# A fused attention and feed-forward kernel: attention output laid over spent columns of the normed x, longer rings, and a new order of the work

## The chip, the cores and the metric

The kernel runs on one core of a Trainium2 chip. The core has several engines that run side by side, each with an instruction stream of its own: TensorE (PE in the profile: matrix multiplications, with weight loads as PEld), VectorE (DVE), ScalarE (ACT), GpSimd (POOL) and SyncE (SP, which here only starts transfers). Sixteen DMA engines move data between the chip's memory (HBM) and the two memories on the core: SBUF, where operands lie, and PSUM, where matmuls leave their sums, in eight banks. Engines wait for one another through semaphores.

The metric is the device time of one execution in microseconds (us), from first to last instruction with what lies around it; smaller is better.

## The reference

From x [1, 2048, 448] in bf16 two branches are computed, from the same normed x, and joined:

```python
xn = layernorm(x)                                   # over the 448 columns
# A: 16 heads of 28, each query sees 8 keys, at distances 0, 2, 4, ... 14 back
q, k, v = split(xn @ wqkv)                          # wqkv [448, 1344]
logits = einsum("bhsd,bhswd->bhsw", q, k[idx]) * 28 ** -0.5   # idx = pos - 2 * arange(8)
o = einsum("bhsw,bhswd->bhsd", softmax(where(idx >= 0, logits, -1e9)), v[idx])
s = o @ wo                                          # wo [448, 448]
# B: feed-forward
h = gelu(xn @ w1 + b1)                              # w1 [448, 1792]
g = silu(h @ w2 + b2)                               # w2 [1792, 448]
out = x + s * g
```

## The kernel before

**Tiling.** Since attention reaches back in steps of 2, even and odd tokens never meet. The kernel sorts them: the first 1024 positions are the even tokens, the second 1024 the odd ones, and within each half the eight keys are neighbours. Positions are cut in 16 tiles of 128 (NT), and 4 chunks of 512 (CH); chunks 0 and 1 are the even half. Attention goes through the positions in 9 visits of 4 x 57 queries.

**Stages.** Each tile of x is loaded, its statistics are taken (`stats`, lines 446 and 451; `rstds`, lines 459 to 469: for the later tiles POOL computes the root and the reciprocal, lines 468 and 469), it is normed (line 481) and transposed into `xnT` (columns by tokens; by TensorE at the start, later by a transposing DMA, line 400). Of it `qk_rows` and `vproj` make queries, keys and values (matmuls of lines 582 and 605), which are cast out of PSUM by ACT (line 334) or by VectorE (line 336). Queries and keys are turned into `qkT` by a transposing DMA (line 400); values go to HBM and back in another layout (line 392). For a visit, `spread` copies keys into `kd` (line 642 on ACT, 644 on VectorE), `scores_of` multiplies (line 757), `weights_of` takes the exponential into a buffer `E` (line 766, ACT) and masks it (line 772, VectorE), and `values_of` multiplies with the values (line 786). `output_of` divides by the sum: transpose (line 795), reciprocal (799), transpose (804), multiply (809), all on VectorE; the multiply writes attention output into `oT` and frees the PSUM bank. The feed-forward runs chunk by chunk: `ff1` (matmul in line 658, gelu on ACT in line 662), then `ff2` (line 690), `gate` (lines 724 to 740) and `final`/`gated` (matmul with wo in line 870, line 897).

**Pairs of half arrays.** The 448 rows that a matmul sums over are 3.5 times 128. `pair` (line 521) therefore runs two jobs beside each other on the upper and the lower 64 rows of the array: a first half of the work for both (four steps of two matmuls), then a second half (three steps of two), in which the two jobs have changed places. Between the two halves TensorE's results of the first must be complete. This is told by a no-op on another engine: it waits for the last matmul of the first half, and the first matmul of the second half waits for it. That engine is POOL:

```python
        def f2(k):
            held["told"] = (nc.gpsimd if k.on == "POOL" else nc.sync).nop()
            for i in held["last"]:
                behind(held["told"], i)
        told = plan.add(HOPS[0] if early else HOPS[1], 0.06, f2, [u], 300)
```

To fill the time between, the halves of neighbouring pairs are interleaved. POOL has other work in the same stream: masks and constants at the start, the roots of lines 468 and 469, some moves of values, and the loads of wo (nine transfers, and two copies within SBUF, issued in line 377 through `dma`).

**What sets the order.** All instructions are first entered as tasks in a plan (`_Plan`). A task has an engine (or a choice of engines, as the casts have, and the moves of values between SP and POOL), a cost, the tasks it depends on, buffers that it takes and gives back, and a priority: a base from `PRIO` by kind and number, plus an entry of `LATER` for the kind of step, plus an entry of `NUDGE` for single tasks by number. The planner plays the tasks through with its costs: among those that can start at about the same time on an engine it takes the one of the highest priority. Buffers are rings (`ring`): `E` has 8, `kd` 2. The instructions are then emitted in the planned order, and each engine runs its own in that order. A changed priority or ring thus moves instructions on all engines, and changes which engine gets a cast, though the code of each step stays.

SP's transfers share eight semaphores in turn, so that each waits for the one eight places ahead of it.

Of the kernel before, what the change touches and what calls it, by code (L numbers as in the profile page):

```python
# [17 lines left out]
TILED = 30  # L18
BURST = 3.5
NUDGE = {  # L20
    140: -82, 155: -215, 164: -68, 167: -111, 224: 188, 279: -38, 288: 225, 645: -245, 658: -217,
    783: -170,
}
LAST = 352
SAME = 20
# [154 lines left out]
def kernel(  # L180
# [13 lines left out]
    P = 128  # L194
    S, D, H, DH, F = A_x.shape[1], 448, 16, 28, 1792
# [4 lines left out]
    KT = 4  # L200
# [5 lines left out]
    G = 4  # L206
    HALF = S // 2


    NW, NK, BACK, PAD = 57, 64, 7, 16  # L210
# [22 lines left out]
    def sb(name, shape, dt=BF16):  # L233
        return const.tile(shape, dt, name=name)
# [10 lines left out]
    b1r = sb("b1r", [P, P])  # L245
    b1 = sb("b1", [P, NMT], F32)
    b2 = sb("b2", [P, D])
    xnT = sb("xnT", [P, KT, S])
    qkT = sb("qkT", [P, 2, G, PAD + S])
    v_tok = [sb(f"v_tok{t}", [P, 2, H // 2, 32]) for t in range(4)]  # L250
    v_hbm = dram.tile([BACK + S, H * 32], BF16, name="v_hbm")
    oT = sb("oT", [P, KT, S])
    o_hbm = dram.tile([NCH, 60, CH], BF16, name="o_hbm")
    ident = sb("ident", [P, P])
    eps_t = sb("eps_t", [P, 1], F32)
# [10 lines left out]
    def ring(name, n, shape, dt=BF16, fifo=False):  # L266
        return _Pool([sb(f"{name}{i}", shape, dt) for i in range(n)], fifo)

    p_xn = ring("xn", 4, [P, 512])
    p_st = ring("st", 4, [P, 6], F32)  # L270
    p_E = ring("E", 8, [P, 8 * NW], fifo=True)
    p_dt = ring("dt", 2, [P, 480], F32)
    p_rd = ring("rd", 2, [P, H], F32)
    p_y = ring("y", 2, [P, D], F32)
# [6 lines left out]
    p_g.bufs = p_g.bufs + late_g  # L281
    p_h = ring("h", 28, [P, CH], fifo=True)
    p_v = ring("v", 3, [P, 4, H // 2, 32], fifo=True)
    p_k = ring("kd", 2, [P, G, 4, 2 * NK], fifo=True)
    qk_tok = [sb(f"qk_tok{i}", [P, 2, H, 32]) for i in range(4)]
    p_f = _Pool([None])
    p_q = _Pool([None] * QUEUE)
# [1 line left out]


    PRIO = {
        "project": (-11.5, -1.5, -311, -502,),
        "project2": (199, 11.5, 108.5, -613,),
        "values": (-78.5, -273, -375.5, -823.5,),
        "attn": (81.5, -4, 22, 86, 131, 124.5, 67, 104, 273,),
        "ff1": (233.5, 220, 157.5, 177, 44.5, 48.5, 44, 141, 160.5, 68.5, 111.5, 100.5, 19, 229.5,
            126.5, 204.5, -15, 453.5, 620, 158, 363.5, 135.5, 189.5, 161.5, 163.5, 118, 129, 171,),
        "gelu": (145, 132, 118.5, 151.5,),
        "ff2": (172.5, -34.5, 266, 114.5, -228.5, 89, -834, 135, 113.5, 180.5, 67.5, 104, -1, 131,
            -15.5, -33.5,),  # L300
        "final": (-5, 2, 130, -16.5, 63, -2, -20, 203, 58, 65.5, 71, 162.5, 202, 134, 31.5, -18,),
        "norm": (131, 11, 219.5, 294, 150, 155.5, 56, 116, 159.5, 154.5, -4.5, 28, 209, 117.5, 66,
            147.5,),
        "pack": (160.5, 13.5, -16, 211.5,),
        "loads": (-194, 474.5, 184.5, 164.5, 124.5, 10.5, -37.5, 238,),
        "stats": (49, 32, 205.5, 205.5, 142.5, 66.5, 114.5, 190, 60, 170.5, 108, 102, 37.5, 179.5,
            65.5, -10.5,),
        "turn_x": (198, 4.5, 200, 12.5, 159, 185, 2, -46.5, 82.5, 172.5, 113, 90, -29, 147.5, -37,
            26,),
        "turn_qk": (67.5, 199, 72, 88.5, 40, 34, 1, 120, 151, 171, 49, -100, 214.5, 171, 176, 181,),  # L310
        "move_v": (216.5, 157, 49, 175.5, 179.5, 58.5, -15.5, 145, -15.5,),
        "store_v": (19, 83.5, -18.5, 87, 75, 196, 82.5, -38, 10, 76, 42.5, 140, 208, 159, 50.5, 50,),
        "spread": (141.5, 2, 192, 29, 156.5, -17.5, 42.5, 178.5, 129.5,),
        "copies": (187, 4, 219, 15.5, 90, 177, 88.5, 31, 29, 20.5, 182, 51, 204.5, 49.5, 24,),
    }
    LATER = {"swap": 679, "qk": 54.5, "v": 156.5, "gelu": -25, "exp": 146.5, "mask": 120.5, "pv": 298, "recip": 205.5, "os": 207, "y": 720.5, "tanh": 162, "g": 22, "sg": 65, "o": 118.5}

    plan = _Plan()

    def buf(pool, owner, i=0):  # L320
        return pool.bufs[owner.slots[pool][i]]

    def pe(n, k=1):
        return k * (n / 2400.0 + 0.0025)

    def act(n):
        return 0.15 + n / 1130.0

    def dve(n, r=1):
        return 0.15 + n / (960.0 * r)  # L330
# [186 lines left out]
    def behind(later, earlier):  # L517
        tc.add_manual_dep(later.ins, earlier.ins.name,
                          mybir.DependencyInfo(mybir.DependencyClass.Sync, mybir.DependencyReason.DATA), reason="row tiles")

    def pair(a, b, prio, early=False, before=(range(4),), after=(range(3),), late=((),), give=()):
# [21 lines left out]
        for i, ks in enumerate(after):  # L543
            def f3(k, ks=ks, n=n, i=i):
                p, q = buf(p_b, t, 0), buf(p_b, t, 1)
                for x in together([part(b, q, kt, 0, n + m) for m, kt in enumerate(ks)], [part(a, p, kt, 1, n + m) for m, kt in enumerate(ks)])[0]:
                    if not i:
                        behind(x, held["told"])
            u = plan.add("PE", pe(a.n, len(ks)), f3, [u if i else told], prio + LATER["swap"], give=give if i + 1 == len(after) else (), tail=0.15, mode=64)
            n += len(ks)  # L550
# [25 lines left out]
    def qk_rows(t, which, prio):  # L576
# [7 lines left out]
        def evac(a, own, i):  # L584
            b = qk_tok[t % len(qk_tok)]

            def fn(k):
                copy(k.on, b[:, which, :, :DH], buf(p_b, own, i)[:, :D].rearrange("p (h c) -> p h c", h=H))
            t_row[t].append(plan.add(("ACT", "DVE"), (act(D), dve(D)), fn, [a, t_qz[t % len(qk_tok)], t_qk.get(t - len(qk_tok))],
                                     prio + LATER["qk"], give=((p_b, own, i),)))  # L590
            if len(t_row[t]) == 2:
# [60 lines left out]
    def ff1(c, mt, prio, gate):  # L652
# [7 lines left out]
        def evac(a, own, i):  # L660
            def fn(k):
                nc.scalar.activation(buf(p_h, own, i)[:], buf(p_b, own, i)[:], ACT.Gelu_apprx_tanh,  # L662
                                     bias=b1[:, mt:mt + 1])
            t_h[(c, mt)] = plan.add("ACT", 0.69, fn, [a, t_b1] + gate, prio + LATER["gelu"],
                                    give=((p_b, own, i),), table=("gelu",))
# [53 lines left out]
    def gate(t, cs, n, a, own, i, biased, prio):  # L719
        if biased:  # L720
            y, pool, at, held = own, p_b, i, ((p_b, own, i),)
        else:
            def f2(k):
                nc.vector.tensor_tensor(out=buf(p_y, k)[:, :n], in0=buf(p_b, own, i)[:, :n], in1=b2[:, cs], op=ALU.add)  # L724
            y, pool, at = plan.add("DVE", dve(n), f2, [a, t_b2], prio + LATER["y"], take=(p_y,), give=((p_b, own, i),)), p_y, 0
            held = ((p_y, y, 0),)
        after = [a, y]

        if t >= NT - TPC:
            def f5(k):  # L730
                nc.scalar.activation(buf(p_g, k)[:, :n], buf(pool, y, at)[:, :n], ACT.Silu)
            t_g[t].append(plan.add("ACT", act(n), f5, after, prio + LATER["tanh"], take=(p_g,), give=held, table=("silu",)))
            return
# [338 lines left out]
```

## Time and profile before

| what | us |
|---|---|
| median of 3 runs (lowest to highest) | 152.66 (152.38 to 152.89) |
| the profiled execution's own time | 153.27 |
| its span, first to last instruction | 151.5 |
| PE busy | 146.4 (97%) |
| DVE busy | 115.5 (76%) |
| ACT busy | 94.8 (63%) |
| POOL busy | 20.9 (14%) |
| matmuls of line 658 (ff1), busy | 44.0 |
| matmuls of line 690 (ff2), busy | 40.5 |
| mean granted TensorE clock | 1.000 |

"Busy" counts the time in which an engine works on at least one instruction. Matmuls overlap: the next begins before the last has ended, so that the time between starts, not the duration of one, says what a matmul costs in a stream. In a timeline each line gives start, length, engine, line, operation, output and inputs, the count, and in brackets how long the engine had been idle and what released it. The chain of waits follows the work that ended last back to its cause at every step.

### The profile page before, as it was taken

What the parts mean: (1) busy time and instruction counts of PE and PEld (TensorE: products, weight loads), DVE (VectorE), ACT (ScalarE), POOL (GpSimd) and SP (SyncE); (2) the same over time, 40 slices, a digit from 0 to 9 for tenths busy, and PEclk for the clock granted to TensorE, in tenths of its full rate; (3) what the DMA queues carried; (4) which work ended last, traced back from release to release, by engine and by line L of the source; (5) the groups of instructions that cost most, each with busy time, mean ns of one, the idle gap of its engine ahead of it and who ended that gap; (6) DMA issues with size and microseconds to landing.
All of it is one profiled execution on the core that took longest, in us unless ns stands there. A gap on an engine that the chain in (4) does not pass through costs nothing.

```text
span 151.5 us, 5233 instructions
## 1 busy us (share of the span) xinstructions
PE 146.4 (97%) x2155; PEld 77.3 (51%) x2155; DVE 115.5 (76%) x278; ACT 94.8 (63%) x166; POOL 20.9 (14%) x57
## 2 busy tenths in 40 slices
PE   7999999999999999999999999999999999999990
PEld 2544444544454555569556554545564444554470
DVE  3886860493647997898699977997799899977871
ACT  3354878458794557979869946893895976302110
POOL 7127330200677200010000000000000000000000
PEclk9999999999999999999999999999999999999999
DMA  4999959779999736339977797423100100141331
GB/s 144 330 301 351 148 120 140 189 209 326 180 173 204 108 74 104 107 107 176 208 178 180 106 125 151 133 83 111 33 4 6 31 13 0 57 130 50 106 95 35
DMA packets 39955, 20.18 MB, mean 133 GB/s; under 512 B 25759, under 2 KB 39254, under 8 KB 39930
## 3 DMA queue, kind: packets, MB, share of 16 engines
q1 hardware_dynamic: 39098, 18.56, 57.6%
q0 software_dynamic: 688, 1.16, 3.8%
q8 instruction: 17, 0.28, 0.8%
q10 hardware_dynamic: 144, 0.11, 0.2%
q14 instruction: 8, 0.07, 0.1%
HBM read 9.65 MB, written 4.19 MB: 91 GB/s over the span
## 4 chain that ended last, share of the span: by engine, by line
PE 82%; DMA 7%; DVE 7%; SPq 1%; issue 1%; ACT 0%
PE bank L658 28%; PE bank L690 24%; PE bank L582 9%; PE bank L870 6%; PE bank L712 4%; DMA w_in<-in_A_wqkv_dram 4%; DMA qkT<-qk_tok 3%; PE bank L605 3%; PE bank L786 3%; PE bank L757 2%; DVE dt L804 2%; DVE dt L795 2%; DVE oT L809 1%; SPq L377 1%; PE bank L878 1%
## 5 line engine op out<-in xcount | busy, mean ns | idle before, releaser
L658 PE MATMUL bank<-xnT,w 64*128 64x512 bf16 x392 | 44.0, 376 | 0.0
L662 ACT ACTIVATE h<-bank,b 128x512 bf16<-128x512 f32 x56 | 34.3, 688 | 12.0 <-PE bank L658 12.0
L690 PE MATMUL bank<-w,h 64*128 64x448 bf16 x392 | 40.5, 349 | 0.0
L658 PEld LDWEIGHTS <-w 64*128 64x128 bf16 x392 | 19.1, 94 | 22.5 <-issue 0.5
L690 PEld LDWEIGHTS <-h 64*128 64x128 bf16 x392 | 18.8, 94 | 16.2
L582 PE MATMUL bank<-w_in,xnT 64*128 64x448 bf16 (+1 forms) x212 | 25.4, 350 | 0.1
L766 ACT ACTIVATE E<-bank 128x456 bf16<-128x456 f32 (+1 forms) x36 | 17.0, 555 | 1.3 <-PE bank L757 1.2
L582 PEld LDWEIGHTS <-xnT 64*128 64x128 bf16 (+1 forms) x212 | 11.3, 94 | 9.3 <-issue 0.9
L334 ACT CAST qk_tok<-bank 128x448 bf16<-128x448 f32 x23 | 11.8, 536 | 6.5 <-PE bank L582 5.2
L605 PE MATMUL bank<-w_in,xnT 64*128 64x448 bf16 (+1 forms) x106 | 14.1, 349 | 0.0
L795 DVE STREAM_TRANSPOSE dt<-bank 128x480 f32<-128x480 f32 (+1 forms) x18 | 12.1, 671 | 1.7 <-PE bank L786 1.6
L772 DVE TENSOR_TENSOR E<-E,m_gen 128x456 bf16<-128x456 bf16 (+1 forms) x32 | 11.6, 389 | 2.0 <-ACT E L766 1.8
L804 DVE STREAM_TRANSPOSE dt<-rd 128x480 f32<-128x480 f32 (+1 forms) x18 | 12.1, 675 | 0.6
L446 DVE BATCH_NORM_STATS2 st<-x_sb 128x6 f32<-128x448 bf16 x16 | 9.6, 608 | 3.8 <-DMA x_sb<-in_A_x_dram 3.7
L809 DVE TENSOR_TENSOR oT<-bank,dt 128x456 bf16<-128x456 f32 (+1 forms) x18 | 11.4, 632 | 0.6
L736 ACT ACTIVATE t<-y 128x448 f32<-128x448 f32 x12 | 6.7, 579 | 7.1 <-DVE y L724 7.1
L724 DVE TENSOR_TENSOR y<-bank,b 128x448 f32<-128x448 f32 x15 | 8.8, 616 | 2.6 <-PE bank L690 2.2
L870 PE MATMUL bank<-wo,oT 64*128 64x448 bf16 x98 | 10.6, 349 | 0.0
L481 DVE TENSOR_SCALAR xn<-x_sb,mv,rstd 128x448 bf16<-128x448 bf16 x16 | 6.3, 396 | 3.1 <-POOL rstd L469 2.9
L605 PEld LDWEIGHTS <-xnT 64*128 64x128 bf16 (+1 forms) x106 | 6.4, 94 | 3.8 <-issue 0.7
L334 ACT CAST v_tok<-bank 128x448 bf16<-128x448 f32 x13 | 6.3, 538 | 1.7 <-PE bank L605 1.1
L644 DVE TENSOR_SCALAR kd<-qkT,head 128x1024 bf16<-128x1024 bf16 x12 | 5.6, 485 | 2.4 <-DMA qkT<-qk_tok 2.3
(79 smaller groups left out, 139.7 us busy)
## 6 DMA issues: line engine op xcount, KB each, us to landing
v<-v_hbm SPq DMA_DIRECT2D x16, 128.0 KB
v_hbm<-v_tok SPq DMA_DIRECT2D x14, 128.0 KB
out_dram<-o SPq DMA_DIRECT2D x15, 112.0 KB
w<-in_B_w_dram SPq DMA_DIRECT2D x2, 672.0 KB
w_in<-in_A_wqkv_dram SPq DMA_DIRECT2D x3, 336.0 KB
x_sb<-in_A_x_dram SPq DMA_DIRECT2D x4, 224.0 KB
w<-in_B_w_dram SPq DMA_DIRECT2D x2, 448.0 KB
w<-in_B_w_dram SPq DMA_DIRECT2D x2, 336.0 KB
```

The source lines that it names most:

```text
L334: nc.scalar.copy(o, i)
L582: return nc.tensor.matmul(ps[:, :D], xnT[r, kt, cs], w, start=start, stop=stop)
L605: return nc.tensor.matmul(ps[:, :D], xnT[r, kt, k0:k0 + P], w, start=start, stop=stop)
L658: return nc.tensor.matmul(ps[:], w1[r, kt, ms], xnT[r, kt, cs], start=start, stop=stop)
L662: nc.scalar.activation(buf(p_h, own, i)[:], buf(p_b, own, i)[:], ACT.Gelu_apprx_tanh, bias=b1[:, mt:mt + 1])
L690: return nc.tensor.matmul(ps[:, :D], buf(*h_at[(c, mt)])[r, cs], w2[r, mt, :], start=start, stop=stop)
L766: nc.scalar.activation(buf(p_E, k)[:, :8 * n], buf(p_b, a, at + i)[:, :8 * n], ACT.Exp, scale=SCALE)
L772: nc.vector.tensor_tensor(out=E, in0=E, in1=m[:, :, :, :n].rearrange("p i g q -> p (i g) q"), op=ALU.mult)
L795: nc.vector.transpose(buf(p_dt, k)[:, :32 * m], buf(p_b, po, i)[:, :32 * m])
L804: nc.vector.transpose(buf(p_dt, d)[:, :32 * m].rearrange("p (b c) -> p b c", c=32), buf(p_rd, r)[:, :m].unsqueeze(2).to_broadcast((P, m, 32)))
L809: nc.vector.tensor_tensor(out=oT[:, a::2, q:q + 4 * n1], in0=buf(p_b, po, i)[:, :n].rearrange("p (l q) -> p l q", l=2), in1=buf(p_dt, d)[: ...
L870: return nc.tensor.matmul(ps[:, :D], oT[r, kt, t * P:(t + 1) * P], wo[r, kt, :], start=start, stop=stop)
```

## The change

`xnT` and `oT` were two tensors of 4 x 2048 columns each. They become two views of one tensor with 4 x 3072: `xnT` is its columns 1024 to 3071, `oT` its columns 0 to 2047. Columns 1024 to 2047 are thus shared: column 1024 + i holds position i of the normed x (the even half, chunks 0 and 1) and, later, position 1024 + i of the attention output (the odd half, from visit 4 on). Of the 8 KB per partition that come free, four more buffers of exponentials (912 bytes each) and a third buffer of spread keys (4 KB) are made. The tables `NUDGE`, `PRIO` and `LATER` are replaced, and so the planned order is another.

```diff
 NUDGE = {
-    140: -82, 155: -215, 164: -68, 167: -111, 224: 188, 279: -38, 288: 225, 645: -245, 658: -217,
-    783: -170,
+    162: -128, 184: 37, 224: 229, 288: 215, 316: -196, 320: -33, 401: 26, 601: 233, 645: -216, 658: -239,
+    683: -22, 716: -130, 784: 236, 786: -67, 818: -201, 855: -33,
 }
...
-    xnT = sb("xnT", [P, KT, S])
+    xT = sb("xT", [P, KT, HALF + S])
+    xnT, oT = xT[:, :, HALF:], xT[:, :, :S]
...
-    oT = sb("oT", [P, KT, S])
...
-    p_E = ring("E", 8, [P, 8 * NW], fifo=True)
+    p_E = ring("E", 12, [P, 8 * NW], fifo=True)
...
-    p_k = ring("kd", 2, [P, G, 4, 2 * NK], fifo=True)
+    p_k = ring("kd", 3, [P, G, 4, 2 * NK], fifo=True)
...
     PRIO = {
-        "project": (-11.5, -1.5, -311, -502,),
-        "values": (-78.5, -273, -375.5, -823.5,),
-        "attn": (81.5, -4, 22, 86, 131, 124.5, 67, 104, 273,),
+        "project": (24.5, 99, -528.5, -741.5,),
+        "values": (-37, -281, -558.5, -888.5,),
+        "attn": (195.5, -26.5, 24.5, 119.5, 122.5, 194.5, 94.5, 151, 281.5,),
...
-    LATER = {"swap": 679, "qk": 54.5, "v": 156.5, "gelu": -25, "exp": 146.5, "mask": 120.5, "pv": 298, "recip": 205.5, "os": 207, "y": 720.5, "tanh": 162, "g": 22, "sg": 65, "o": 118.5}
+    LATER = {"swap": 796, "qk": 34.5, "v": 25.5, "gelu": 177, "exp": 131.5, "mask": 30, "pv": 254.5, "recip": 157.5, "os": 155.5, "y": 1290, "tanh": 55, "g": -6, "sg": 65, "o": 122.5}
```

The other rows of `PRIO` change in the same way. Two lines more stand ahead of the functions, so line 809 of before is line 811 after, and so on. In the emitted streams the numbers of operations are almost the same: TensorE has 2155 matmuls in both; three casts out of PSUM go from VectorE (33 to 30) to ACT (39 to 42); one store of values goes from SP to POOL. All else is a change of place: on POOL, one load of wo stands between the fourth and fifth of the seven no-ops of the run of ff1 in chunk 1, five between the fifth and sixth, and one before the seventh, where before all of them stood behind the seventh; at the start 16 instead of 14 whole-array matmuls precede the first 64-row pair; on VectorE, spreads, masks and the steps of `output_of` are interleaved in another way.

More of the change, by code (lines that the diff above doesn't have):

```diff
@@ L291 @@
     PRIO = {
-        "project": (-11.5, -1.5, -311, -502,),
-        "project2": (199, 11.5, 108.5, -613,),
-        "values": (-78.5, -273, -375.5, -823.5,),
-        "attn": (81.5, -4, 22, 86, 131, 124.5, 67, 104, 273,),
[L296 to L313, printed above, removed]
+        "project": (24.5, 99, -528.5, -741.5,),
+        "project2": (4.5, -53.5, 79.5, -758,),
+        "values": (-37, -281, -558.5, -888.5,),
@@ new lines @@
+        "attn": (195.5, -26.5, 24.5, 119.5, 122.5, 194.5, 94.5, 151, 281.5,),
+        "ff1": (187.5, 92.5, -0, 126.5, 135, 49.5, 7, 85, 134, 27.5, 182, 22, -7.5, 50.5, 183.5,
+            21, -47, 164.5, 111.5, 188, 99, 167.5, 193, 95.5, 91.5, 150, 128, 53,),
+        "gelu": (-8.5, 193, 21.5, 53.5,),
+        "ff2": (151, -34.5, 3.5, 114.5, -60, 89, -953.5, 135, 109.5, 180.5, 128, 104, -7.5, 131,
+            -31, -286.5,),
+        "final": (31, 2, -25.5, -16.5, 30, -2, 51, 203, 222, 65.5, -12.5, 162.5, 148.5, 134, -74.5,
+            170.5,),
@@ new lines @@
+        "norm": (131, 11, 219.5, 294, 136.5, 46, 31, 10.5, 13.5, 7.5, -18.5, -29, 195, 92, 55.5, 6,),
+        "pack": (193.5, -2.5, 170, 67,),
+        "loads": (20, 2.5, 66.5, 212, 40.5, 39, 79, 139,),
+        "stats": (49, 32, 205.5, 205.5, 218, 295.5, 187.5, -6, 183.5, 95.5, 138.5, 20, 151, 152.5,
+            -6.5, -38,),
+        "turn_x": (198, 4.5, 200, 12.5, 67.5, 133, 84, 56.5, 27, 188.5, 173.5, 37.5, 96, 46, 133.5,
+            175.5,),
+        "turn_qk": (71.5, 82, 125, 51, 49, -6, 194, 15.5, 95.5, 206.5, 124, 98.5, 162.5, 58, 97.5,
+            92,),
@@ L314 @@
+        "move_v": (19, 156.5, -16, 126, 58, 182, 106, 94, 103.5,),
+        "store_v": (161.5, 189.5, 216.5, 179, -16, 28.5, 64, 74.5, 227.5, 201.5, 82, 181.5, -17,
+            153.5, 172, 2.5,),
+        "spread": (39, 218, 151.5, 119, 49.5, 137, 56.5, 179.5, 124.5,),
         "copies": (187, 4, 219, 15.5, 90, 177, 88.5, 31, 29, 20.5, 182, 51, 204.5, 49.5, 24,),
     }
-    LATER = {"swap": 679, "qk": 54.5, "v": 156.5, "gelu": -25, "exp": 146.5, "mask": 120.5, "pv": 298, "recip": 205.5, "os": 207, "y": 720.5, "tanh": 162, "g": 22, "sg": 65, "o": 118.5}
+    LATER = {"swap": 796, "qk": 34.5, "v": 25.5, "gelu": 177, "exp": 131.5, "mask": 30, "pv": 254.5, "recip": 157.5, "os": 155.5, "y": 1290, "tanh": 55, "g": -6, "sg": 65, "o": 122.5}
```

## The prediction

> **What bounds the kernel now.** I read the page first: spans and busy shares.
>
> ```profile
> span 151.5 us, 5233 instructions
> PE 146.4 (97%) x2155; PEld 77.3 (51%) x2155; DVE 115.5 (76%) x278; ACT 94.8 (63%) x166; POOL 20.9 (14%) x57
> PEclk9999999999999999999999999999999999999999
> PE 82%; DMA 7%; DVE 7%; SPq 1%; issue 1%; ACT 0%
> ```
>
> TensorE is busy 97% of the span at full clock, and 82% of the chain that ended last is its work. Its number of matmuls stays 2155, so the change can only win what TensorE loses between matmuls. I looked for that in the timeline, by the start-to-start times of neighbouring matmuls: a pair of 64-row matmuls with 448 columns takes 0.189 us (L690 x392 in line 690's long runs), one with 512 columns 0.216. From 11.5 us to the last matmul at 147.7 all runs together lie 2.95 us above such packing. About half of it is changes of shape (0.095 us each time that 64-row and 128-row matmuls alternate, 0.105 around each of the nine passes of line 786), which stay. Some 1.3 us are waits: 0.08 at 72, 0.19 at 79, 0.48 at 83.5, 0.2 at 92.3, 0.15 at 108, the rest diffuse. The largest, in the timeline:
>
> ```profile
> 81.84 0.25 DVE L799 RECIPROCAL rd<-dt 128x15 f32<-128x15 f32 x1
> 82.12 0.68 DVE L804 STREAM_TRANSPOSE dt<-rd 128x480 f32<-128x480 f32 x1
> 82.81 0.54 PE L757 MATMUL bank<-qkT,kd 64*128 64x56 bf16 x17
> 82.84 0.63 DVE L809 TENSOR_TENSOR oT<-bank,dt 128x456 bf16<-128x456 f32 x1
> 83.52 0.36 PE L757 MATMUL bank<-qkT,kd 64*128 64x56 bf16 x15 [0.18 <-DVE oT L809]
> ```
>
> The 17 score matmuls need 17 x 0.43/32 = 0.23 us (the chain has "85.21 0.43 PE bank L757 x32"), so the next was due at 83.04; it began at 83.52, 0.04 after the multiply of line 809 freed its bank. The chain of waits shows what made that multiply late:
>
> ```profile
> 67.76 5.25 DMA qkT<-qk_tok
> 73.01 0.02 issue
> 73.03 0.49 DVE kd L644
> 73.53 0.92 DVE E L772 x3
> 74.45 0.60 DVE dt L795
> ...
> 82.84 0.64 DVE oT L809
> 83.48 0.04 issue
> 83.52 0.36 PE bank L757 x15
> ```
>
> A transposing DMA lands at 73.01; then VectorE works without a hole for 10.45 us: one spread, three masks, four times transpose, reciprocal, transpose, multiply (0.60+0.26+0.69+0.63 and gaps, 2.26 each). POOL matters in one place, where TensorE hands over through it:
>
> ```profile
> 37.66 0.31 POOL L468 TENSOR_SCALAR sd<-mv,eps_t 128x4 f32<-128x4 f32 x1 [7.08 <-DVE mv L451]
> 38.04 1.04 POOL L469 TENSOR_TENSOR rstd<-sd,half_t 128x4 f32<-128x4 f32 x1
> 40.36 3.08 POOL L377 DMA_DIRECT2D wo<-in_A_wo_dram  x5 [1.28 <-PE bank L658]
> ...
> L538 POOLq EVENT_SEMAPHORE  x1: 17/17/17, 39.7 to 39.7; - x1
> ```
>
> (The last line is the answer on line 538 for 39 to 41 us.) Five loads of wo issue back to back in 3.08 us (0.70, 0.61, 0.59, 0.60, 0.60). They stand behind the last handover of that stretch of ff1 (the no-op of line 538 at 39.71), beside long halves of line 690: nobody waits.
>
> **The change, part by part.** The profiled execution took 153.27 us: 151.5 of span and 1.77 around it, 0.61 above the median 152.66. I sum against it and carry the difference to the median.
>
> *Layout.* Attention output in columns 1024 to 2047 overlies columns of the normed x that chunks 0 and 1 read; those readers are the ff1 matmuls of chunks 0 and 1 and their projections, which stand ahead of the writing visits (4 on) in both orders. No instruction is added: 0, and no wait that the order did not have. The 8 KB go to four more exponential buffers and one more of spread keys. No wait of before ends in "a buffer of E came free", so the ring alone is worth 0; what it allows shows only through the order.
>
> *Start.* Now 16 whole-array matmuls of lines 582 and 605 precede the first 64-row pair, instead of 14. Before, TensorE had a pair at 9.59, then stood from 9.78 to 9.89 for the second piece of w_in3: 0.116. Two more at 0.189 put the pair at about 9.97, behind that landing: -0.12. But whole-array and 64-row batches then alternate five times instead of three: 2 x 0.095 = +0.19. Sum +0.07. The Trainium skill, "TensorEngine Tiling (Array Packing)", Key Properties, says a change of tiling mode drains TensorE; if that meant a matmul's whole 0.35 less its 0.19 spacing, the two switches would be +0.32 and the start +0.20. The row has 0.095, which decides.
>
> *POOL.* In the changed order the four-tile rstd (0.31 + 1.04, with gaps 1.46) goes ahead of the fourth handover of ff1 in chunk 1, one wo load between the fourth and fifth of the seven, five between the fifth and sixth, one before the seventh, two behind. From the end of the half whose handover precedes the five, TensorE has 28 matmuls at 0.108 = 3.02 us (L658 x46 in 4.97 us), then wants the next handover. Counted from its last matmul's start: needed at 0.216 + 3.02 = 3.24. The handover before comes at 0.42 (0.376 of matmul, 0.04 of signal: 39.29 to 39.71); the first issue appears 0.65 later (39.71 to 40.36), the fifth 0.60+0.60+0.58+0.63 = 2.41 behind it. If the next no-op must wait until the fifth has begun, it comes at 3.48, and with 0.06 to TensorE the stall is +0.30, with the 0.70 of a first issue +0.40. If POOL's sequencer runs ahead of these issues, it is 0. The trace shows both habits without deciding: the no-op at 38.20 is served 0.15 after line 469 began, not 0.9 later at its end, so ends are not awaited; none is seen ahead of a queue of five. The Trainium skill, "Perfetto Trace Analysis", DMA Instruction — SWDGE (GPSIMD), lets the sequencer take the next instruction once the issue is pushed to a wait queue: by it, 0. I take the middle, +0.2, and keep 0 and +0.4. The wo copies (0.56 each) now stand ahead of the second ff2 handover: last wo lands about 48, copies end about 49.3, wanted at 50.3; cover 1 us.
>
> *VectorE at 79 and 83.* Three casts go to ACT (0.54 there, 0.62 here; ACT is 63% busy and stood idle 1.14 us at 78.4, before two such casts): 1.86 us less VectorE work in all, but only what lies between 73.03 and 83.48 shortens that chain, and there all four blocks stay. The third kd buffer lets a spread go earlier, and the last two multiplies stand together. I see 0.1 to 0.2 of chain gone, and TensorE arrives later by whatever POOL costs it. 83.5: from 0 to -0.48, I take -0.25. 79: from 0 to -0.19, taken at -0.1.
>
> *92 to 108.* The wait at 92.3 (0.2, on line 809) goes, as 84 instead of 64 ff1 matmuls of line 658 run before the next line-786 pass and the chain behind is earlier; but there banks are freed by gelus (0.69 each, line 662) and by line 724 (0.62), and at 96 one ff1 half wants a bank right as a line-724 add ends: +0.2. Net 0, ends -0.2 and +0.2. 108 (0.15, on an exponential): exponentials are allowed further ahead, -0.05, ends -0.15 and 0.
>
> *Queues.* One v_hbm store moves from SP to POOL: 0.57 of issue at about 70, where POOL is idle; it stands ahead of two handovers whose cover is over 0.3. The x loads of tiles 12 to 15 precede w2 on SP. Tail: same order, 0.
>
> Sum: +0.07 + 0.2 - 0.25 - 0.1 + 0 - 0.05 = -0.13: 153.14 profiled, 152.53 at the median; I say 152.5. All good ends together: +0.07 - 0.48 - 0.19 - 0.2 - 0.15 = -0.95, 151.7. All bad ends: +0.07 + 0.4 + 0.2 = +0.67, 153.3.
>
> **Rivals.**
> *A, faster:* POOL's sequencer runs ahead of the five issues (stall 0) and the waits at 79, 83.5, 92 and 108 go, with the new one at 96 no more than half: -0.85, 151.8. For it: the no-op served beside line 469. Against: if TensorE isn't delayed at 40 it comes to 83 sooner and meets the same bank, so the two gains partly exclude each other.
> *B, slower:* a transposing DMA of the chain at 67 to 73 lands late. It took 5.25 there and 3.1 where it was alone; the order of SP's transposes, v loads and stores around it is new. Behind it 10.45 us of VectorE have no slack, or 0.2 by my estimate, so each us costs 0.8 to 1. From 0.7 late on the result is slower than before by over 0.3%; 1.2 late (half the spread of 2.15 between those latencies) gives +1.0 - 0.13 = +0.9, 153.5.
> *C, the order is not used:* the same data limits in front of TensorE with new labels; ±0.1, 152.6: within the forecast.
>
> **How the numbers follow.** 0.3% is 0.46 us, about what a measurement can tell from no change. Forecast with C, 0.40: 152.1 to 153.1. A, 0.31. B and other late transfers, 0.29. Range: a third of A lies below 151.7, a fifth of B above 153.8; 151.7 to 153.8 leaves out under 0.2.
>
> **What would show it.** Line 658 without a hole near 39.8 clears POOL; one of 0.3 to 0.4, with its weight load waiting on a POOL sequencer, proves the stall. L757 at 83.5 as an unbroken x32 shows the gain; a bank still waiting for line 811 (809 before) shows none. The first 64-row pair near 9.97, without a wait, and five switches of 0.095 behind. I am wrong if L790 to L812 begin over 0.7 us later than 74.4, or if rstd's x tiles land after 35 and POOL's fourth handover waits.

## The result and the profile after

The changed kernel is slower: 153.95 us at the median (152.38 to 154.63, 20 runs) against 152.46 for the kernel before (152.08 to 153.41, 20 runs); the ratio, taken over all runs, is 1.0074, with a 95% interval of 1.0048 to 1.0100, or 1.1 us, less than the 1.49 between the medians. Its times fall into two groups with a gap between them: 5 of the 20 lie from 152.38 to 152.72, 15 from 153.23 to 154.63. The profiled execution (154.19 us, span 152.5) is of the upper group.

The page, with the shares of busy time:

```profile
span 152.5 us, 5234 instructions
PE 145.0 (95%) x2155; PEld 75.6 (50%) x2155; DVE 113.1 (74%) x275; ACT 95.6 (63%) x169; POOL 21.4 (14%) x58
```

TensorE has less busy time than before (146.4) and yet a longer span. The timeline of TensorE shows the three places that the prediction spoke of (start, length, instruction, count, idle time before with its releaser):

```profile
30.07 10.74 PE L660 MATMUL bank<-xT,w 64*128 64x512 bf16 x98
82.39 0.58 PE L759 MATMUL bank<-qkT,kd 64*128 64x56 bf16 x32
96.14 1.04 PE L660 MATMUL bank<-xT,w 64*128 64x512 bf16 x8 [1.02 <-DVE y L726]
```

The run of ff1 past 39 us is whole: 98 matmuls, no hole, so POOL's five loads stalled no matmul. The score matmuls at 82.39 are an unbroken 32: the wait of 0.48 at 83.5 is gone. So are those at 79, 92 and 108. But at 96.14 TensorE stood for 1.02 us. The waits of TensorE and VectorE (total, times, longest) say for what:

```profile
PE bank L660 <- DVE y L726: 1.0, 1, 1.0
...
DVE kd L646 <- DMA qkT<-qk_tok: 4.1, 2, 2.6
```

TensorE waited for a bank that VectorE's add in line 726 frees; VectorE in turn had waited 2.6 us for a transposing DMA in front of its spreads of keys (line 646). The chain of waits goes back to SP:

```profile
85.85 1.31 SPq L402
...
87.73 0.30 SPq L850
...
88.07 2.04 SPq L850
...
90.84 3.07 DMA qkT<-qk_tok
...
93.94 0.89 DVE kd L646 x2
94.83 0.55 DVE w_in L742
...
95.46 0.64 DVE y L726
...
96.14 1.02 PE bank L660 x7
```

On SP, five small copies of attention output (line 850, HBM to SBUF) stand behind one transposing DMA and ahead of the next. The third took 2.04 us to issue where the others took 0.30 to 0.47, so the second transposing DMA was issued at 90.84 and landed 3.07 later. In the order before, it stood ahead of three of these copies, but its own issue took 2.91, and it landed no earlier. SP, VectorE and TensorE of before:

```profile
89.07 2.91 SPq L400 DMA_TRANSPOSE qkT<-qk_tok  x1
...
93.87 0.89 DVE L644 TENSOR_SCALAR kd<-qkT,head 128x1024 bf16<-128x1024 bf16 x2 [1.04 <-DMA qkT<-qk_tok]
...
95.40 0.62 DVE L724 TENSOR_TENSOR y<-bank,b 128x448 f32<-128x448 f32 x1
...
88.86 7.46 PE L658 MATMUL bank<-xnT,w 64*128 64x512 bf16 x64
96.25 0.70 PE L786 MATMUL bank<-E,v 64*32 64x57 bf16 x64
96.88 0.39 PE L658 MATMUL bank<-xnT,w 64*128 64x512 bf16 x2
```

There too the two spreads waited for the landing and the add stood behind them; it ended at 96.02, against 96.09 after. It did no harm because TensorE, behind a pass of line 786, came to the 65th matmul of its ff1 run only at 96.88. After, the run begins 0.91 earlier and goes on past 64 without such a pass: the 65th was due at about 94.97, 0.216 behind the pair before it. So between these two profiles it is not the landing that moved but the moment at which TensorE wants the bank.

Summed as the prediction did, by the time between the starts of matmuls, TensorE lies above packing, from 11.5 us to the last matmul: 2.95 us before and 2.95 after. The run of 84 matmuls around 96 took 10.46 us from its first start to the start of what follows, where the same run without a stall (in the next profile of this kernel, below) takes 9.16. So 1.3 of the 2.95 after is this one stall, and 1.65 is left where before had 2.95.

So up to the last matmul the profiled runs are even (147.69 and 147.53). What differs is behind it, a part of the program that looks alike in both. The last two steps of VectorE before, then after:

```profile
147.84 0.26 DVE L890 TENSOR_TENSOR sg<-bank,w_in 128x96 bf16<-128x96 f32 x1
148.13 0.21 DVE L897 TENSOR_TENSOR o<-x_sb,sg 128x96 bf16<-128x96 bf16 x1
```

```profile
147.99 0.26 DVE L892 TENSOR_TENSOR sg<-bank,w_in 128x96 bf16<-128x96 f32 x1 [0.26 <-issue]
148.28 0.21 DVE L899 TENSOR_TENSOR o<-x_sb,sg 128x96 bf16<-128x96 bf16 x1
```

After, VectorE stood 0.26 us for nothing that the profile shows ("issue"). Then the DMA view of 2.5 us from the issue of the last store (40 slices of 0.0625 us), before from 148.36 and after from 148.52:

```profile
GB/s 0 0 0 0 0 0 158 259 327 270 271 135 23 0 55 148 133 56 3 0 0 0 0 0 0 0 0 0 0 0 0 0 0 0 0 0 0 0 0 0
...
q1 hardware_dynamic: 288, 0.11, 17.2%
```

```profile
GB/s 0 146 237 304 270 226 147 23 0 131 0 0 0 74 168 127 45 11 0 11 11 11 0 9 15 0 0 0 0 0 0 0 0 0 0 0 0 0 0 0
...
q1 hardware_dynamic: 288, 0.11, 18.1%
q14 instruction: 1, 0.01, 0.8%
```

Both stores (88 KB and 24 KB) show as two humps. Behind the second, after has a trickle of some 11 GB/s for another 0.5 us, and a queue that before does not have in this stretch: one packet of 8 KB of instructions. Before has such a packet too, but it starts ahead of the stretch. The landings of the sixteen shares of each store tell the same:

| | before | after |
|---|---|---|
| last matmul ends | 147.69 | 147.53 |
| last store issued | 148.36 | 148.52 |
| the 8 KB of instructions | 148.11 to 148.63 | 149.12 to 149.43 |
| 88 KB store: 15th share, 16th share | 149.57, 149.57 | 149.42, 150.56 |
| 24 KB store: 15th share, 16th share | 149.85, 149.86 | 149.96, 150.75 |
| span ends | 151.47 | 152.49 |
| last matmul to end of span | 3.78 | 4.96 |

After, the packet of instructions runs while the first store does, and one share of sixteen comes 1.14 us behind the other fifteen; the end of the program waits for it. The Trainium skill, "DMA: Bandwidth & Descriptors", Queues, rings and completion order, says that a DMA engine serves its queues in turn and finishes a whole packet of one before it turns to the next; the trace agrees in that only one share is late, but the packet took 0.31 us and the share lost 1.14, so it is not the whole account.

### The profile page after: what moved, and what is told of

It reads as the page before. It is cut to its first block, busy times and chain, and to the rows that moved or that the text cites. A ratio compares the mean times of both kernels' runs of the same rounds, so it can differ in the third digit from the quotient of the medians.

```text
span 152.5 us, 5234 instructions
## 1 busy us (share of the span) xinstructions
PE 145.0 (95%) x2155; PEld 75.6 (50%) x2155; DVE 113.1 (74%) x275; ACT 95.6 (63%) x169; POOL 21.4 (14%) x58
## 4 chain that ended last, share of the span: by engine, by line
PE 82%; DMA 6%; SPq 4%; DVE 2%; ACT 2%; issue 1%; DVEq 0%; ACTq 0%
PE bank L660 24%; PE bank L692 22%; PE bank L584 14%; PE bank L607 7%; PE bank L872 6%; DMA w_in<-in_A_wqkv_dram 4%; PE bank L788 3%; PE bank L714 3%; SPq L850 2%; PE bank L759 2%; DMA qkT<-qk_tok 2%; ACT E L768 2%; SPq L379 1%; PE bank L880 1%; SPq L402 1%
## 5 line engine op out<-in xcount | busy, mean ns | idle before, releaser
L660 PE MATMUL bank<-xT,w 64*128 64x512 bf16 x392 | 43.9, 376 | 1.0 <-DVE y L726 1.0
L692 PE MATMUL bank<-w,h 64*128 64x448 bf16 x392 | 40.0, 349 | 0.0
L660 PEld LDWEIGHTS <-w 64*128 64x128 bf16 x392 | 20.3, 94 | 22.2 <-issue 1.6
L692 PEld LDWEIGHTS <-h 64*128 64x128 bf16 x392 | 18.3, 94 | 16.4
L584 PE MATMUL bank<-w_in,xT 64*128 64x448 bf16 (+1 forms) x212 | 24.5, 350 | 0.3 <-DMA w_in<-in_A_wqkv_dram 0.3
L584 PEld LDWEIGHTS <-xT 64*128 64x128 bf16 (+1 forms) x212 | 10.4, 94 | 10.3 <-issue 0.9
L336 ACT CAST qk_tok<-bank 128x448 bf16<-128x448 f32 x25 | 12.3, 539 | 4.7 <-PE bank L584 4.1
L607 PE MATMUL bank<-w_in,xT 64*128 64x448 bf16 (+1 forms) x106 | 13.3, 350 | 0.0
L811 DVE TENSOR_TENSOR xT<-bank,dt 128x456 bf16<-128x456 f32 (+1 forms) x18 | 10.6, 614 | 0.2
L872 PE MATMUL bank<-wo,xT 64*128 64x448 bf16 x98 | 10.6, 349 | 0.0
L338 DVE CAST qk_tok<-bank 128x448 bf16<-128x448 f32 x7 | 4.3, 625 | 6.7 <-PE bank L584 6.7
```

The source lines that it names most:

```text
L336: nc.scalar.copy(o, i)
L584: return nc.tensor.matmul(ps[:, :D], xnT[r, kt, cs], w, start=start, stop=stop)
L607: return nc.tensor.matmul(ps[:, :D], xnT[r, kt, k0:k0 + P], w, start=start, stop=stop)
L660: return nc.tensor.matmul(ps[:], w1[r, kt, ms], xnT[r, kt, cs], start=start, stop=stop)
L692: return nc.tensor.matmul(ps[:, :D], buf(*h_at[(c, mt)])[r, cs], w2[r, mt, :], start=start, stop=stop)
L811: nc.vector.tensor_tensor(out=oT[:, a::2, q:q + 4 * n1], in0=buf(p_b, po, i)[:, :n].rearrange("p (l q) -> p l q", l=2), in1=buf(p_dt, d)[: ...
```

## The experiments

Two causes were under test, called M and E in the expectations (E is T in the two runs that looked for it on SP). **M**: in the middle, the copies on SP make a transposing DMA late, and VectorE's stream in that order hands the delay to TensorE. **E**: at the end, a change in the length of some engine's stream moves the fetch of instructions and holds VectorE. The rivals were the layout and rings themselves, the casts, and a gain that never came. Each run is compared with runs of the kernel before on the same chip. In the diffs, `place(n, ref, k)` takes task n out of the planned order and puts it before (k = 0) or behind (k = 1) task ref.

**The changed kernel, unaltered.**

> The changed kernel once more, unaltered, for a second profile and as the mark for the next three on one chip. Two places carry its loss in the first profile: TensorE stands 1.02 us near 95 (line 660 waits for the add of line 726), and the last two stores of the output complete 0.9 us later than before, because one of the sixteen shares of the first comes 1.1 us behind the other fifteen. If both places are part of the order: about 153.9 us again, and both are seen again. If they were chance of that one execution: one of them or both are gone from the profile, while the time stays spread between 152.4 and 154.6.

153.63 us (152.30 to 154.03), ratio 1.0048 [1.0020, 1.0076]. The two groups came back: 3 of 12 from 152.30 to 152.58, 9 from 153.45 to 154.03. The profiled execution (152.58, span 150.8) is one of the lower group; SP, VectorE and TensorE in its timeline:

```profile
86.69 2.47 SPq L850 DMA_DIRECT2D xT<-o_hbm  x5
89.21 1.24 SPq L402 DMA_TRANSPOSE qkT<-qk_tok  x1
...
92.31 0.89 DVE L646 TENSOR_SCALAR kd<-qkT,head 128x1024 bf16<-128x1024 bf16 x2 [1.09 <-DMA qkT<-qk_tok]
...
87.99 9.23 PE L660 MATMUL bank<-xT,w 64*128 64x512 bf16 x84
```

The same five copies took 2.47 us here and 3.58 in the profile of after (87.22 to 90.80); the spreads came 1.63 earlier, and 84 matmuls ran without a hole. TensorE's excess over packing is 1.64, so against the profile of before the order wins 1.3 us where the stall stays away. The end is long all the same: 4.51 from the last matmul to the end.

**One transposing DMA ahead of four of the five copies** (M alone is undone):

```diff
+    place(487, 914, 0)
+    place(488, 487, 1)
```

> One move on SP's queue: the transposing DMA into qkT that stands behind five small copies of line 850 (issued at 90.84, landed at 93.91) goes ahead of them. Theory M: the third of these copies takes 2.04 us to issue behind the transposing DMA in front, so the five hold the next one, its late landing holds the two spreads of line 646, and they hold the add of line 726 behind them in VectorE's queue, which frees TensorE's bank. Then the landing comes at about 92, the stall at 95 shrinks from 1.0 to 0.2 or less, and the time falls by 0.7 to 1.0 us to about 153.0. Rival: the landing is late for contention among the DMA engines, wherever it stands in the queue; then the landing moves by under 0.5, and the time stays within 0.3 of the changed kernel's.

152.76 us, from 152.25 to 153.18: no upper group any more. Ratio 1.0003 [0.9981, 1.0026].

```profile
87.96 1.91 SPq L402 DMA_TRANSPOSE qkT<-qk_tok  x1
89.91 1.50 SPq L850 DMA_DIRECT2D xT<-o_hbm  x4
...
87.52 9.23 PE L660 MATMUL bank<-xT,w 64*128 64x512 bf16 x84
```

The transposing DMA now goes ahead of four copies, it lands 0.46 us earlier than in the profile above, and TensorE has no hole. The end stays at 4.73.

**VectorE's two spreads behind the add of line 726** (the same cause cut at its other end; SP is left alone):

```diff
+    for n in (808, 807):
+        place(n, 607, 1)
```

> The changed kernel with one move on VectorE: the two spreads of line 646 that wait for the late transposing DMA go behind the add of line 726. Theory M: the landing stays as late as it was in many executions (92.3 to 93.9), but the add no longer waits for it, so TensorE does not stand at 95, the slow group of times (153.5 to 154.5) is gone, and the median is 152.4 to 152.9. Rival: the spreads, now later by 0.6, delay the scores behind them and a stall of 0.5 to 1 appears at 104 or later; the median stays above 153.4.

152.66 us, from 152.33 to 153.34, ratio 1.0004 [0.9986, 1.0023]. This is the clearest of these runs, since in its profile the copies on SP were slow again:

```profile
86.55 3.39 SPq L850 DMA_DIRECT2D xT<-o_hbm  x5
89.99 1.24 SPq L402 DMA_TRANSPOSE qkT<-qk_tok  x1
...
91.59 0.62 DVE L726 TENSOR_TENSOR y<-bank,b 128x448 f32<-128x448 f32 x1
93.08 1.69 DVE L646 TENSOR_SCALAR kd<-qkT,head 128x1024 bf16<-128x1024 bf16 x4 [0.86 <-DMA qkT<-qk_tok]
...
87.71 9.23 PE L660 MATMUL bank<-xT,w 64*128 64x512 bf16 x84
```

The copies took 3.39 and the DMA landed at 93.05, but the add that frees the bank ran at 91.59, ahead of the spreads, and TensorE ran through. So the late transfer harms only by what is queued behind its waiter on VectorE: that half of M is shown. That the copies on SP are what makes it late is shown less well, as the next run's profile tells.

**Four more handovers told on SP as well** (between 103 and 117 us; SP's stream 216 to 221 instructions, where before had 219), which asks whether the packet at the end is SP's:

```diff
+            if 103.0 < k.start < 117.5:
+                held["more"] = nc.sync.nop()
+                for i in held["last"]:
+                    behind(held["more"], i)
...
+                        if "more" in held:
+                            behind(x, held["more"])
```

> Four handovers of line 540 between 104 and 117 us, where SP has little to do, are told on SP as well as on POOL: SP's stream becomes five instructions longer (221 instead of 216), nothing else moves. Theory T: the late share of the last store comes from an 8 KB instruction fetch (149.12 to 149.43) on one DMA engine, made when SP reaches a certain place in its stream; in the kernel before, whose SP stream is three instructions longer, the same fetch comes at 148.11 to 148.63, before the last stores move data at 148.74. With five more it comes near 148 or earlier: the last two stores complete 0.7 to 0.9 us earlier, the time falls by about 0.8 to 153.1. Rival: the fetch belongs to another engine or falls by chance; then it stays near 149.1, the late share too, and the time is that of the changed kernel within 0.3.

153.52 us, ratio 1.0036 [1.0005, 1.0066]. The packet still started 1.13 behind the last matmul, the last store took 2.20 to land, and the end 4.74: SP's stream is not what decides. Its profile also has the stall near 96, with quick copies:

```profile
86.46 2.29 SPq L856 DMA_DIRECT2D xT<-o_hbm  x5
88.80 1.48 SPq L402 DMA_TRANSPOSE qkT<-qk_tok  x1
...
93.69 0.89 DVE L652 TENSOR_SCALAR kd<-qkT,head 128x1024 bf16<-128x1024 bf16 x2 [2.62 <-DMA qkT<-qk_tok]
...
95.89 2.33 PE L666 MATMUL bank<-xT,w 64*128 64x512 bf16 x20 [0.98 <-DVE y L732]
```

The five copies took 2.29 and the transposing DMA was issued at 88.80, earlier than in the second profile of the changed kernel (89.21), which has no stall; but it took 4.9 us to land instead of 3.1. So the landing can be late without a slow copy. In the five profiles of the changed order that leave SP's order at this place alone it comes at 92.3 to 93.9; in the four that move the DMA ahead of the copies, at 91.8 to 93.1. The move helps, and does not settle it.

The same with the transposing DMA moved as well:

> Both edits together. If M and T hold and are independent: 1.6 to 1.9 us less than the changed kernel, about 152.1, that is 0.2 to 0.4 faster than the kernel before, since the waits of before at 79, 83.5, 92 and 108 stay away. If only one holds: about 153.0. If neither: about 153.9.

154.39 us, ratio 1.0082 [1.0044, 1.0119], and a miss that the edit itself made: SP was held in a copy when TensorE wanted its handover, as the waits show.

```profile
PE bank L698 <- SPq L544: 2.0, 1, 2.0
```

Its end, 4.40, is one of the long ones too; its time says nothing more.

**The kernel before with the layout alone, then with layout and rings** (old tables, so old order):

```diff
-    xnT = sb("xnT", [P, KT, S])
+    xT = sb("xT", [P, KT, HALF + S])
+    xnT, oT = xT[:, :, HALF:], xT[:, :, :S]
...
-    oT = sb("oT", [P, KT, S])
```

> The kernel before, with the attention output laid over the spent columns of the normed x and nothing else: rings of 8 and 2, the old tables, so the old order and the old number of instructions on every engine. Both theories: the layout costs nothing, 152.5 to 152.8, within 0.3% of before. If the shared columns made waits: slower, with waits of line 809 on ff1's matmuls. Its profile is also a second look at the end of before's order: theory E (the end of the changed order is slower because of where an 8 KB instruction fetch falls) expects 1.5 us from the last store's issue to its landing, as before; if it takes 1.8 to 2.2 here too, the end is chance.

152.83 us, ratio 1.0001 [0.9981, 1.0021]; the end 3.76, as before. With 12 and 3 buffers in the rings besides:

> The kernel before with the overlay and the longer rings (12 and 3), and the old tables: what the freed room gives by itself, since the planner may now start exponentials and spreads earlier. If the rings were what mattered: faster by 0.3 to 1 us, with the waits at 83.5 or 108 gone. If the order by the tables is what mattered: within 0.5 of before, the waits near 79 to 92 moved but not gone.

152.47 us, ratio 0.9998 [0.9973, 1.0023], and the wait at 83 stands where it stood:

```profile
82.36 0.54 PE L757 MATMUL bank<-qkT,kd 64*128 64x56 bf16 x17
83.07 0.36 PE L757 MATMUL bank<-qkT,kd 64*128 64x56 bf16 x15 [0.17 <-DVE xT L809]
```

Neither layout nor rings cost or bring anything; all of the change is in the order and the three casts that go with it.

**The kernel before with three casts on ACT.** In the emitted streams VectorE's is 330 instructions long before and 328 after (three casts less, one wait more; the page counts only those that do work, 278 and 275). Here nothing but the engine of three casts near 12, 18 and 28 us is changed, which makes it 326:

```diff
+    for n in (186, 200, 276):
+        task(n).on = "ACT"
```

> The kernel before, old order and old rings, with one thing that the change does: three casts of line 336 (two near 12 to 18 us, one near 28) go from VectorE to ACT. VectorE's stream falls from 330 to 326 instructions. Theory E: the end is now as in the changed order, though nothing else changed: the last line-890 product starts about 0.3 us later behind TensorE's last matmul, the 8 KB fetch comes behind the last store's issue, and that store lands 1.8 to 2.2 us after its issue instead of 1.5; the time rises by 0.5 to 0.9 us above before, to 153.2 to 153.6. Rival: the end follows from the order of the work or from chance; then 152.5 to 152.8 as before.

153.60 us, ratio 1.0071 [1.0045, 1.0098]: as much slower as the whole change. TensorE's excess stays at 2.80, near the 2.95 of before, and the end grows to 4.57. **The same with four fills of an unused tile on VectorE near 23 us**, which makes 330 again:

```diff
+    spare = sb("spare", [P, 4], F32)
+    for n in range(4):
+        plan.add("DVE", 0.06, lambda _, n=n: nc.vector.memset(spare[:, n:n + 1], 0.0), [], 0)
```

> The kernel before with the three casts on ACT, as in the run above that was 0.7% slower, and four fills of an unused tile on VectorE near 23 us, where it is idle: the work is that of the slower kernel and four fills more, but VectorE's stream has 330 instructions again. Theory E: the end is that of before (last store lands 1.5 us after its issue), the time 152.4 to 152.8, within 0.3% of before. Rival: moving the casts costs by itself (ACT later, or its casts in the way); then the time stays at 153.4 to 153.7.

152.70 us, ratio 0.9988 [0.9960, 1.0016]; the end 3.82. The DMA views of the 2.5 us from the last store's issue, without and with the fills:

```profile
GB/s 0 0 0 56 180 293 293 390 192 68 11 0 0 65 157 108 40 23 34 23 11 9 15 0 0 0 0 0 0 0 0 0 0 0 0 0 0 0 0 0
...
q14 instruction: 1, 0.01, 1.5%
```

```profile
GB/s 0 0 0 0 0 0 158 259 315 259 282 147 23 0 37 154 142 56 6 0 0 0 0 0 0 0 0 0 0 0 0 0 0 0 0 0 0 0 0 0
...
q1 hardware_dynamic: 288, 0.11, 17.3%
```

Without the fills the trickle and the packet are there, with them neither in this stretch. The casts are the same in both, so it is not they that lengthen the end but the number of instructions on VectorE.

**The changed kernel with the fills, without and with the moved transposing DMA** (332 and 331 instructions):

> The changed kernel with only the four fills on VectorE near 23 us (332 instructions). Theory E: its end becomes that of before (last line-892 product without the 0.3, last store 1.5 us after its issue), while the random stall at 95 stays: times in two groups, near 151.9 and near 153.1, each 0.7 to 0.9 below the changed kernel's groups, median 152.9 to 153.2 or, with few slow ones, lower. Rival: median as the changed kernel's, 153.6 to 153.9.

153.31 us, ratio 1.0027 [1.0002, 1.0051]. The last store landed in 1.47 again, but the hold of 0.3 on VectorE had only moved to an earlier product, so the end was 4.21, and with M left in, both groups remained (5 of 12 up to 152.85, 7 from 153.28). Less was won than expected: the lower group is no lower than that of the unaltered kernel.

> The transposing DMA ahead of the copies, as in the run before, and four small fills of an unused tile on VectorE near 23 us, where it is idle: its stream is 331 instructions long instead of 327 (330 in the kernel before). Theory E with the fetch made by VectorE: the fetch of 8 KB comes four instructions earlier, ahead of the last two stores as in the kernel before (about 0.4 us behind TensorE's last matmul, not 1.2), the last store lands 1.5 us after its issue instead of 2.2, and the time falls from 152.76 to 152.1 to 152.3. Rival: the fetch stays 1.1 to 1.3 us behind the last matmul, and the time at 152.8.

152.10 us, ratio 0.9968 [0.9939, 0.9996]; the end 3.87. Ten of its times lie from 151.79 to 152.42, but two at 153.4, and its profile still had 0.39 of the stall at 95.35, with a landing at 93.1.

**All three: DMA moved, spreads moved, fills.**

> The changed kernel with the three edits that helped: transposing DMA ahead of the copies, the two spreads behind the add of line 726, four fills on VectorE. Both theories together: no stall near 95, the end as before, TensorE's last matmul near 146.0, median 151.7 to 152.0, 0.5% faster than the kernel before, with a narrow spread. If the landing is late in other ways, or the edits get in each other's way: 152.1 as with two of them.

151.97 us (151.44 to 152.58), ratio 0.9962 [0.9940, 0.9984]: faster than both kernels.

TensorE's excess, counted from its first run of ff1, is 1.64, and the end 3.86. The -1.3 in the middle alone would give more than the 0.6 measured. In this profile the stretch ahead of the first run of ff1 lay 1.4 us above packing, against 0.8 in that of before; it scatters from 0.5 to 1.4 among the profiles of the changed order, and there is one profile per kernel, so where the rest went in the other runs stays open.

From the last matmul to the end, all twelve runs and the two kernels fall apart at one place: 3.76 to 3.87 with 329, 330 or 331 instructions on VectorE, 4.40 to 4.96 with 326 to 328, and 4.21 with 332, where only the hold is left. The late share goes with it: in all seven profiles with 326 to 328 one of the sixteen shares of the 88 KB store lands 0.7 to 1.1 behind the other fifteen, and in all seven with 329 and more the sixteen lie within 0.21.

## Why the prediction was wrong

It said 152.5, with 151.7 to 153.8 as the range. The measured 153.95 lies outside, on the slower side, by two things that pull up and one that pulls down further than I had it.

*"Tail: same order, 0"* is the first step that failed. The order of the tail is the same, but its time is not: it grew by 0.7 to 1.2 us, 0.9 in the mean of the six runs with 326 to 328 instructions and no spoiled edit (4.71 against 3.79 in the four profiles of the old order with 329 or 330). I had counted the three casts that leave VectorE as 1.86 us less work and looked no further; a slowdown as large as the whole one can be had from them alone (run with three casts on ACT, 1.0071).

*"92 to 108"* is the second, and failed in its size. It named the right place and the right wait, "at 96 one ff1 half wants a bank right as a line-724 add ends", and priced it at +0.2. Without the stall it was 0; with it 1.3, in about three of four executions if the upper group of times is the stall (24 of 32 times of the changed kernel lie above 153.2; one profile of each group bears it out). What I did not follow is what stands in front of that add on VectorE: two spreads that wait for a transposing DMA. The rows of before held most of it: the add ended at 96.02, and 64 matmuls at 0.108 from 88.86 make the 65th due at 95.77, or 95.42 after the 0.35 that the sum itself won at 79 and 83.5. That is 0.6 of stall, not 0.2, and what TensorE gained beyond the sum made it 1.1.

Rival B had a transposing DMA late with VectorE without slack behind it, but between 67 and 73 us, and later than in the kernel before. In the two first profiles it was as late before (spreads at 93.87) as after (93.94), and only the slack behind it was gone. That B's 153.5 lies near the result is luck. (Its 1.2 us is called half of 2.15, which is 1.08.)

*VectorE at 79 and 83.5* was taken at -0.35 of at most -0.67, with 108 at -0.05. All of it went, and with the waits at 92 and the diffuse part the excess fell by 1.3 (2.95 to 1.64), where my best case allowed 1.0. So of rival A's condition the waits gone was met and the one at 96 was not, and its 151.8 is about what the changed kernel gives once the two faults are mended (151.97).

*POOL*, +0.2 with ends 0 and +0.4, was 0. The profile's POOL rows of after, and the answer on the no-op's line for 39 to 41 us:

```profile
34.73 1.04 POOL L471 TENSOR_TENSOR rstd<-sd,half_t 128x4 f32<-128x4 f32 x1
...
37.17 4.83 POOL L379 DMA_DIRECT2D wo<-in_A_wo_dram  x8 [0.72 <-PE bank L660]
...
L540 POOLq EVENT_SEMAPHORE  x2: 17/17/17, 39.2 to 39.9; - x2
```

The five issues began at 37.17, 37.87, 38.47, 39.04 and 39.59; the no-op behind all five was served at 39.25, 0.21 after the fourth and 0.34 before the fifth. Its matmuls had ended near 38.7, so it was delayed, but by one issue less than I reckoned; the weight load behind it waited 0.30 for it, but the matmul after that load was due at 39.35 and began then. The cover was about 0.05 us.

*Start*: +0.07 by the sum; over the profiles the stretch up to the first run of ff1 is 0.76 above packing in five of the old order and 0.85 in nine of the new, +0.09, with a scatter of 0.4 to 1.4 that hides it in any one run. *Layout* and *rings alone*: 0, as said, and measured at 1.0001 and 0.9998.

The terms as measured: -1.3 for the waits, +0.1 at the start, +1.3 in three of four for the stall, +0.9 at the end, together +0.7; the mean difference is 1.13 with an interval of 0.7 to 1.5, so up to 0.4 is not accounted for.

Shown: the stall, that it goes when the add no longer waits behind the spreads, the end's dependence on the number of instructions on VectorE, that layout and rings are neutral. Only argued: that the late share is late because of the packet of instructions, since no run moved the packet by itself, and that the hold of VectorE has the same origin. Open: why the transposing DMA lands 1.6 us later in one execution of the same kernel than in another (its copies ahead took 2.47 and 3.58 us to issue, but in one profile it was late behind quick copies), and why the end was long with 326 to 328 and partly with 332, but not between.

## What to carry to other kernels

Before a move is priced at nothing, read the in-order queue of each engine at the place where it lands: not only what the moved instruction waits for, but which releases stand behind it, down to a DMA on SP that the one in front waits for. A transfer that lands just as late as before can cost time once another engine has lost its slack behind it; so when a move makes an engine earlier, work out again what it will now wait for. When a kernel's times fall into two groups, profile one of each: here the gap led to one wait. And compare the time from the last matmul to the end of the span as a row of its own; where it moves although its work has not, try a few idle instructions on the engine whose stream changed in length.

## What the runs showed of the hardware

A stream's length was worth about 0.7%: three casts fewer on VectorE at 12 to 28 us cost 0.9 us (153.60 against 152.66), 0.8 of it behind the last matmul by the profiles, and four fills of an unused tile gave it back (152.70 against 152.79). What goes with it in the profile is a packet of 8 KB of instructions that starts 0.32 to 0.48 us behind the last matmul with 329 and more instructions, and 1.13 to 1.58 behind it with 328 and fewer, and a last store that lands in 1.45 to 1.51 or in 1.79 to 2.23.

The third small copy that stands on SP behind a transposing DMA took 2.04 us to issue in one execution of the changed kernel and 0.59 in another, with nothing changed in the program. The transposing DMA behind the five landed 3.1 us after its issue in both, and 4.9 in a run whose copies were quick.
